# Linear attention and a squared-ReLU FFN on one core: another load order, PE transposes for two batches, and row modes in groups

## The chip, the core and the metric

One core of a Trainium2 chip runs the whole kernel. Its engines work side by side: TensorE (PE in the profile, with PEld for its weight loads), VectorE (DVE), ScalarE (ACT), GpSimd (POOL) and SyncE (SP), the last two also issuing DMAs. The metric is device time in microseconds of one execution, the median of three runs: 383.3 us before (382.87 to 383.75).

## What is computed

```python
def phi(x):
    proj = np.einsum('bhsd,df->bhsf', x, w_phi)
    proj = proj - np.max(np.abs(proj), axis=-1, keepdims=True)
    return np.concatenate([np.exp(proj), np.exp(-proj)], axis=-1)
q_p, k_p = (phi(q), phi(k))
kv = np.einsum('bhsf,bhsd->bhfd', k_p, v)
z = np.sum(k_p, axis=2)
num = np.einsum('bhsf,bhfd->bhsd', q_p, kv)
den = np.einsum('bhsf,bhf->bhs', q_p, z)[..., None] + 1e-06
x = (num / den).transpose(0, 2, 1, 3).reshape(B * S, H * D)
h = np.maximum(x @ w_in, 0.0)
out = h * h @ w_out
```

8 batches, 8 heads, 576 positions, head size 64, 128 features; then 4608 tokens of width 512 through an FFN of width 2048. Inputs and output are float32; the kernel computes in bfloat16 with float32 sums.

## The kernel before

Everything is recorded first as operations of a `Plan` (L46): engine, estimated cost, a key (its priority), the operations that it needs, and the buffers that it takes from rings. `Plan.order` (L78) then walks through estimated time and gives each free engine, among the operations that are ready and find their buffers free, the one with the lowest key. The instructions are written in that order, and each engine runs its own in order. `fill` (L51) puts a warming matmul on PE whenever it has nothing to do before the first transposed tile (`warm`, L321, two matmuls of 128 columns).

Attention runs batch by batch (`attention`, L342). The names, with their lines:

- Loads (L294 to L319): GpSimd issues the DMAs of k, q and v (tiles xk, xq, xv), in halves for batch 0, and of the two FFN weights, win and wout.
- Transposes of k and q to kT and qT (L347): on PE with copies by ScalarE or VectorE (L364, L372, L375) for batch 0 and for k of batch 1, else by DMA from SyncE's queue (L353). NPE at L180 sets which.
- The k side: in five groups, PE projects k (L412), VectorE takes the largest absolute value (mk, L423) and, from batch 1 on, subtracts it (ksh, L433), ScalarE makes both exponentials (kph, L441; in batch 0 L454). In batch 0 v is scaled instead (va, L461 and L467, half on VectorE and half on GpSimd). PE sums kph times va in two halves (L500), which are copied to kv_sb (L513, L517).
- The q side, in blocks of 64 positions, two at a time and at the end of a batch one alone: PE projects (L538, features in rows; L567, positions in rows), ScalarE takes exponentials (qph, L548), VectorE the maximum (m, L571), GpSimd moves it to the place of its rows (mq, L580), ScalarE makes em of it (L587). PE makes numerators and denominators in two steps (L616), with a multiplication by em on VectorE between them (L627); VectorE divides (rden L634, xo L638).
- xo is transposed to xT by PE (L648, L653) in batch 0 and by DMA later (L657).

The FFN runs on chunks of four token tiles of 128: `ffn_in` (L669) makes 512 columns of hidden values with PE (L679), ReLU on ScalarE (hr, L684) and the square on GpSimd or VectorE (L687, L690); `ffn_out` (L699) sums with wout (L708), VectorE copies (ot, L715), SyncE stores (L720). The first chunk's FFN-in units take one tile at a time and then two; all others take four at once (L730 to L740).

Matmuls of the projections and of the sums over k use PE in row halves (64\*128 in the profile, `rows=64` in the plan); the others use all rows. The numerators of a single block write only 64 rows of PSUM (128\*64 in the profile).

Of the kernel before, what the change touches and what calls it, by code (L numbers as in the profile page):

```python
# [45 lines left out]
class Plan:  # L46
# [30 lines left out]

    def order(self):  # L78
# [13 lines left out]
        while True:  # L92
            for e, q in ready.items():
# [3 lines left out]
                while q:  # L97
                    it = heapq.heappop(q)
                    o = it[2]
# [58 lines left out]
def kernel(  # L158
# [10 lines left out]
    nc = tc.nc  # L169
# [10 lines left out]
    NPE = 2  # L180
# [15 lines left out]
    ones = sb.tile([P, Fd], BF16, name="ones")  # L196
# [24 lines left out]
    NATT, LEAD, DUE, SPAN = 6, 3, 34, 28  # L221

# [71 lines left out]
    def loads(b, dep=None):  # L294
        got = {}
        for i, (name, src, r) in enumerate((("k", k, r_xk), ("q", q, r_xq), ("v", v, r_xv))):
            buf = Buf(r)
            rows = src[b].rearrange("h s d -> (h s d)").rearrange(
                "(pr t c) -> t pr c", pr=NPR, t=P)

            def fn(a, z, buf=buf, rows=rows):
                nc.gpsimd.dma_start(
                    out=buf.t[:, a * NJ : z * NJ].rearrange("t (pr j) d -> t pr (j d)", j=NJ),
                    in_=rows[:, a:z, :],
                )
            key = FIRST + i if b == 0 else FIRST + (10, 13, 14)[i] if b == 1 else 32 * b - 120
            cut = (0, 2, 4) if b == 0 else (0, 4)
            got[name] = buf, [[load(key, 295 * (z - a), 128 * (z - a),
                                    lambda a=a, z=z, fn=fn: fn(a, z), [dep], [buf])]
                              for a, z in zip(cut, cut[1:])]  # L310
        return got

    x0 = loads(0)
    o_id = pool(FIRST + 0.5, 700, lambda: make_identity(nc, ident))
    win_v = moe_w_in.rearrange("(kc p) m -> p kc m", p=P)
    wout_v = moe_w_out.rearrange("(kc p) n -> p kc n", p=P)
    o_win = load(FIRST + 5, 4194, 512, lambda: nc.gpsimd.dma_start(out=win, in_=win_v))
    x1 = loads(1)
    o_wout = load(FIRST + 12, 4194, 2048, lambda: nc.gpsimd.dma_start(out=wout, in_=wout_v))  # L319

    def warm():  # L321
        for _ in range(2):
            nc.tensor.matmul(out=r_one.tiles[7][:, :P], lhsT=ones, rhs=ones, start=True, stop=True)  # L323
# [18 lines left out]
    def attention(b, x, key):  # L342

        (xk, lk), (xq, lq), (xv, lv) = x["k"], x["q"], x["v"]
        kT, qT = Buf(r_kT), Buf(r_qT)

        def transposes(xb, ld, xt, at):  # L347

            ops = []
            if b >= NPE or b and at:  # L350
                for u0, n in GRP:
# [5 lines left out]
                    ops.append(xbar(key(at), n * 16, fn, ld[0] + (x["v"][1][0] if b > 1 else []), [xb, xt]))  # L357
# [167 lines left out]
        for i, (g0, j0, nj) in enumerate(order_j):  # L525
# [19 lines left out]
            for bk in range(2):  # L545
                for t, sg in zip(qg, (1.0, -1.0)):
                    def fn(w=w, t=t, sg=sg, nj=nj, bk=bk):
                        nc.scalar.activation(  # L548
                            out=t.t.rearrange("f pr hi p -> f (pr hi p)")[:, : nj * 512].rearrange(
                                "f (r b c) -> f b r c", r=2, b=2)[:, bk],  # L550
                            in_=w[bk].t[:, : nj * 256].rearrange("f (r c) -> f r c", r=2),
                            func=ACT.Exp, scale=sg)
                    qe.append(act(kk, nj * 256, fn, [p_], [w[bk], t]))
# [23 lines left out]
            def move(m0=m0, mq=mq, nj=nj, lo=lo):  # L577
                for jj in range(nj):
                    for hi in range(2):
                        nc.gpsimd.tensor_copy(  # L580
                            out=mq.t[lo + jj * 64 : lo + jj * 64 + 64, :, :, hi],
                            in_=m0.t[hi * 64 : hi * 64 + 64, :, : 2 * nj].rearrange(
                                "x b (r j) -> x r b j", j=nj)[:, :, :, jj])
# [220 lines left out]
```

## Time and profile before

| what | us |
|---|---|
| median of three runs | 383.3 |
| span of the profiled execution, first to last instruction | 382.5 |
| around it, against the median | 0.8 |
| PE busy, of which warming matmuls | 366.7, 24.0 |
| VectorE, ScalarE, GpSimd busy | 247.7, 244.4, 185.9 |
| first FFN-in matmul | 37.45 |
| first FFN-out matmul | 49.49 |

The only profile is that of one execution; its span stands for that execution's time. In rows of the timeline the columns are: start, length, engine, line, operation, tiles written and read, array mode and shapes, count, and in brackets the engine's idle time just before and what ended it. A row's length for several matmuls runs to the modelled end of the last one; the distance between two rows' starts tells what the first one cost PE.

### The profile page before, as it was taken

The page shows a single profiled execution, that of the slowest core. Times are in us where ns is not written, and L with a number is a line of the kernel's source. Part 1 is how long each engine was busy: PE and PEld are TensorE (multiplying, and loading weights), DVE is VectorE, ACT ScalarE, POOL GpSimd, SP SyncE. Part 2 cuts the span into 40 slices and gives each one's busy share as a digit, 9 for nine tenths or more (in the row PEclk, how much of TensorE's full clock was granted, in tenths as well). Part 3 has the DMA queues.
Part 4 walks back from the last instruction along what each step waited for, and adds up shares of the span by engine and source line. Part 5 has one row for each costly group of instructions (what it writes and reads, how often), then busy time and mean ns, then how long its engine had stood idle before and what let it go on. Part 6 is the DMA issues. An engine that isn't in the chain of part 4 may idle for free.

```text
span 382.5 us, 10585 instructions
## 1 busy us (share of the span) xinstructions
PE 366.7 (96%) x4194; PEld 200.9 (53%) x4194; DVE 247.7 (65%) x554; ACT 244.4 (64%) x485; POOL 185.9 (49%) x317
## 2 busy tenths in 40 slices
PE   8989999978999999999999999999999999999994
PEld 8868857544544454545543544455446444444442
DVE  1857894899279738973699488956895843333221
ACT  3785788649972986489758974996399733333300
POOL 8533766507890986079728674677446420000000
PEclk9998999999999999999999999999999999999998
DMA  7999994257944595459665946495631422112123
GB/s 114 213 208 205 162 174 73 48 91 133 195 50 89 91 217 62 80 105 202 99 85 109 169 85 104 91 196 102 105 77 30 71 55 49 35 29 55 27 64 75
DMA packets 70721, 40.41 MB, mean 106 GB/s; under 512 B 51088, under 2 KB 65552, under 8 KB 70672
## 3 DMA queue, kind: packets, MB, share of 16 engines
q1 hardware_dynamic: 55360, 21.38, 31.2%
q0 software_dynamic: 15312, 18.35, 29.4%
q8 instruction: 33, 0.54, 0.6%
q14 instruction: 16, 0.13, 0.1%
HBM read 36.77 MB, written 9.44 MB: 121 GB/s over the span
## 4 chain that ended last, share of the span: by engine, by line
PE 74%; DMA 11%; DVE 9%; issue 3%; POOL 1%; DVEq 0%; POOLq 0%
PE one L708 32%; PE one L679 25%; DMA wout<-in_moe_w_out_dram 8%; PE one L616 5%; PE one L500 5%; DVE mk L423 4%; DVE ksh L433 3%; PE one L538 3%; DMA xv<-in_v_dram 2%; PE one L567 2%; PE one L412 2%; DVE ot L715 1%; DVE xo L638 1%; POOL va L467 1%; DVE one L627 1%
## 5 line engine op out<-in xcount | busy, mean ns | idle before, releaser
L687 POOL TENSOR_TENSOR h<-hr 128x512 bf16<-128x512 bf16 x112 | 115.2, 1042 | 83.7 <-ACT hr L684 81.7
L679 PE MATMUL one<-xT,win 128*128 128x512 bf16 (+2 forms) x704 | 144.2, 341 | 2.8 <-DVE ksh L433 2.8
L708 PE MATMUL one<-wout,h 128*128 128x512 bf16 x576 | 144.5, 380 | 0.8 <-DMA wout<-in_moe_w_out_dram 0.5
L684 ACT ACTIVATE hr<-one 128x512 bf16<-128x512 f32 x144 | 84.5, 603 | 67.7 <-PE one L679 59.8
L548 ACT ACTIVATE qph<-one 128x512 bf16<-128x512 f32 (+1 forms) x160 | 77.9, 563 | 19.5 <-PE one L538 19.3
L679 PEld LDWEIGHTS <-win 128*128 128x128 bf16 x704 | 59.2, 98 | 54.6 <-issue 3.5
L708 PEld LDWEIGHTS <-h 128*128 128x128 bf16 x576 | 51.0, 98 | 56.6 <-issue 1.4
L441 ACT ACTIVATE kph<-ksh 128x1024 bf16<-128x1024 f32 (+1 forms) x70 | 64.8, 964 | 19.7 <-DVE ksh L433 19.2
L571 DVE TENSOR_REDUCE m<-one 128x4 f32<-128x512 f32 (+1 forms) x80 | 47.9, 630 | 41.7 <-PE one L567 24.9
L423 DVE TENSOR_REDUCE mk<-one 128x4 f32<-128x512 f32 (+1 forms) x80 | 49.7, 627 | 8.3 <-PE one L412 8.2
L433 DVE TENSOR_TENSOR ksh<-one,mk 128x512 f32<-128x512 f32 (+1 forms) x70 | 44.7, 638 | 3.8
L715 DVE COPY ot<-one 128x512 f32<-128x512 f32 x36 | 24.7, 685 | 28.2 <-PE one L708 28.0
L580 POOL COPY mq<-m 64x4 f32<-64x4 f32 x144 | 26.5, 184 | 32.0 <-DVE m L571 27.3
L616 PEld LDWEIGHTS <-qph 128*128 128x128 bf16 (+1 forms) x640 | 29.7, 100 | 22.2 <-issue 11.3
L616 PE MATMUL one<-kv_sb,qph 128*128 128x65 bf16 (+1 forms) x640 | 36.9, 196 | 1.5 <-DVE one L627 1.4
L627 DVE TENSOR_TENSOR one<-one,em 128x260 f32<-128x260 f32 (+1 forms) x80 | 31.5, 429 | 5.8 <-PE one L616 2.3
L638 DVE TENSOR_TENSOR xo<-one,rden 128x256 bf16<-128x256 f32 (+1 forms) x80 | 31.7, 419 | 0.8
L690 DVE TENSOR_TENSOR h<-hr 128x512 bf16<-128x512 bf16 x32 | 13.5, 423 | 24.4 <-ACT hr L684 24.4
L323 PE MATMUL one<-ones 128*128 128x128 bf16 x316 | 24.0, 236 | 1.1 <-DVE scrap L281 1.1
L500 PE MATMUL one<-va,kph 64*128 64x65 bf16 x1152 | 22.8, 191 | 0.9 <-issue 0.9
L500 PEld LDWEIGHTS <-kph 64*128 64x128 bf16 x1152 | 20.5, 94 | 4.3 <-issue 3.3
L323 PEld LDWEIGHTS <-ones 128*128 128x128 bf16 x316 | 20.6, 106 | 2.5 <-DVE scrap L281 1.1
(43 smaller groups left out, 184.5 us busy)
## 6 DMA issues: line engine op xcount, KB each, us to landing
out_dram<-ot SPq DMA_DIRECT2D x72, 128.0 KB, 2.4
xk<-in_k_dram POOLq DMA_DIRECT2D x7, 576.0 KB, 6.1
xq<-in_q_dram POOLq DMA_DIRECT2D x7, 576.0 KB, 9.8
xv<-in_v_dram POOLq DMA_DIRECT2D x7, 576.0 KB, 12.2
win<-in_moe_w_in_dram POOLq DMA_DIRECT2D x1, 2048.0 KB, 18.5
wout<-in_moe_w_out_dram POOLq DMA_DIRECT2D x1, 2048.0 KB, 32.4
xk<-in_k_dram POOLq DMA_DIRECT2D x2, 288.0 KB, 5.6
xq<-in_q_dram POOLq DMA_DIRECT2D x2, 288.0 KB, 7.6
```

The costliest lines, as they stand in the source:

```text
L323: nc.tensor.matmul(out=r_one.tiles[7][:, :P], lhsT=ones, rhs=ones, start=True, stop=True)
L423: nc.vector.tensor_reduce(out=mk.t[:, e, ms], in_=wv(e), axis=AX.X, op=ALU.max, apply_absolute_value=True)
L433: nc.vector.tensor_tensor(out=ksh.t[:, e, : n // 2, :], in0=wv(e), in1=mk.t[:, e, ms].to_broadcast([P, n // 2, Fd]), op=ALU.subtract)
L441: nc.scalar.activation(out=t.t[:, :, : n // 2, :].rearrange("x e i f -> x e (i f)"), in_=ksh.t[:, :, : n // 2, :].rearrange("x e i f -> x ...
L500: nc.tensor.matmul(out=kvp(w, hi)[:, 2 * prl + s], lhsT=kph[g][s].t[r, i % 2, i // 2, :], rhs=va[s].t[r, u, : D + 1], start=(j == 0), stop ...
L548: nc.scalar.activation(out=t.t.rearrange("f pr hi p -> f (pr hi p)")[:, : nj * 512].rearrange("f (r b c) -> f b r c", r=2, b=2)[:, bk], in ...
L571: d1 = [dve(kk, nj * 256, lambda w=w, m0=m0, nj=nj, bk=bk: nc.vector.tensor_reduce(out=m0.t[:, bk, : 2 * nj], in_=w[bk].t[:, : nj * 256].r ...
L616: nc.tensor.matmul(out=nd(slice(0, D + 1))[:, z], lhsT=qg[s].t.rearrange("f pr hi p -> f (pr hi p)")[:, h * (hi_ - lo) : (h + 1) * (hi_ - ...
L679: nc.tensor.matmul(out=w.t[:, y * n : (y + 1) * n], lhsT=win[:, kc, mc * P : (mc + 1) * P], rhs=xT.t[:, a:z, kc, :], start=(kc == 0), stop ...
L684: o = act(key - 4, TCH, lambda: nc.scalar.activation(out=r.t, in_=w.t, func=ACT.Relu), [p_], [w, r])
L687: o = pool(key - 4, 1050, lambda: nc.gpsimd.tensor_tensor(out=t.t, in0=r.t, in1=r.t, op=ALU.mult), [o], [r, t])
L708: nc.tensor.matmul(out=w.t, lhsT=h2[c, mc, tt][0].t[:, h2[c, mc, tt][1] :][:, :P], rhs=wout[:, mc, :], start=(mc == 0), stop=(mc == KC2 - 1))
```

## The change

1. The loads are issued in the order k0, v0, q0, win, k1, v1, wout, q1 (the digit is the batch), and later batches in the order k, v, q.
2. NPE becomes a pair, and q of batch 1 is transposed by PE as well.
3. The second chunk's FFN-in units take two token tiles instead of four: first all eight units of its first two tiles, then those of the other two.
4. A new `pick` chooses for PE between operations that use row halves and the others, so that several of one kind follow each other.
5. Numerators of a single block are made for all 128 columns of qph, of which 64 are used; qph is laid out for that.
6. In batch 0 em comes straight from the maxima, with four small ScalarE operations instead of GpSimd's four copies and one.
7. One warming matmul of 256 columns stands for two of 128.

```diff
+    AHEAD, GROUP, LATE = 12, 2, 4
+
+    def pick(self, q, rows, can):
+        now = min((it[0] for it in q if it[2].rows == 128), default=None)
+        half = sorted(it for it in q if it[2].rows == 64 and can(it[2]))
+        if now is None or now < 1 or not half:
+            return None
+        if rows == 64:
+            go = half[0][0] < now + self.AHEAD
+        else:
+            go = half[0][0] < now - self.LATE or (
+                len([it for it in half if it[0] < now]) >= self.GROUP)
+        if go:
+            one = half[0]
+        else:
+            one = min((it for it in q if it[2].rows == 128 and can(it[2])), default=None)
+            if one is None:
+                return None
+        q.remove(one)
+        heapq.heapify(q)
+        return one
...
-                while q:
-                    it = heapq.heappop(q)
-                    o = it[2]
+                one = self.pick(q, rows[e], can) if e == "pe" else None
+                while q or one:
+                    it = one or heapq.heappop(q)
+                    one, o = None, it[2]
...
-    NPE = 2
+    NPE = 2, 2
...
+    EMB = 1
...
+    FIRSTS = "k0 v0 q0 win k1 v1 wout q1"
...
+    def loads(b, dep):
+        for name in "kvq":
+            load_x(b, name, 32 * b - 120, dep)
...
     def warm():
-        for _ in range(2):
-            nc.tensor.matmul(out=r_one.tiles[7][:, :P], lhsT=ones, rhs=ones, start=True, stop=True)
+        nc.tensor.matmul(
+            out=r_one.tiles[7][:, : 2 * Fd], lhsT=ones[:, :P], rhs=ones, start=True, stop=True)
...
-            if b >= NPE or b and at:
+            if b >= NPE[at]:
...
+            if b < EMB:
+                def fn(m0=m0, em=em, nj=nj, lo=lo):
+                    for jj in range(nj):
+                        for hi in range(2):
+                            nc.scalar.activation(
+                                out=em.t[lo + jj * 64 : lo + jj * 64 + 64].rearrange(
+                                    "x (r b hi) -> x r b hi", r=2, b=2)[:, :, :, hi],
+                                in_=m0.t[hi * 64 : hi * 64 + 64, :, : 2 * nj].rearrange(
+                                    "x b (r j) -> x r b j", j=nj)[:, :, :, jj],
+                                func=ACT.Exp, scale=-2.0)
+                o_em = act(key(20), 200, fn, d1, [m0, mq, em])
...
                         nc.tensor.matmul(
-                            out=nd(slice(0, D + 1))[:, z],
-                            lhsT=qg[s].t.rearrange("f pr hi p -> f (pr hi p)")[
-                                :, h * (hi_ - lo) : (h + 1) * (hi_ - lo)],
+                            out=w.t[:, z * P : z * P + D + 1],
+                            lhsT=qg[s].t[:, h // 2, h % 2, :],
...
+        if c == 1:
+            ins = [(0, c, (i, a, a + 2)) for a in (0, 2) for i in range(8)]
```

Three places in the orders of instructions show what moves. The first is GpSimd's queue after its constants, with the first loads; in it L302 and L328 load k, q and v, L317 and L343 load win, L319 and L346 load wout, and L467 and L500 scale v. Before:

```order
L302 DMA xk_69<-in_k_dram 128x2x576 x2
masks.py:197 MEMSET ident 128x128
masks.py:199 ISA
masks.py:199 AFFINE_SELECT ident<-ident 128x128
L302 DMA xq_71<-in_q_dram 128x2x576 x2
L302 DMA xv_73<-in_v_dram 128x2x576 x2
L317 DMA win<-in_moe_w_in_dram 128x4x2048
L302 DMA xk_70<-in_k_dram 128x4x576
L302 DMA xq_72<-in_q_dram 128x4x576
L302 DMA xv_74<-in_v_dram 128x4x576
L467 TENSOR_TENSOR va_91<-xv_73,va_91 128x8x64 x2
L319 DMA wout<-in_moe_w_out_dram 128x16x512
```

and now, from the second half of k0 on:

```order
L328 DMA xk_69<-in_k_dram 128x2x576
L328 DMA xv_73<-in_v_dram 128x2x576 x2
L328 DMA xq_71<-in_q_dram 128x2x576 x2
L343 DMA win<-in_moe_w_in_dram 128x4x2048
L328 DMA xk_70<-in_k_dram 128x4x576
L328 DMA xv_74<-in_v_dram 128x4x576
L500 TENSOR_TENSOR va_91<-xv_73,va_91 128x8x64
L346 DMA wout<-in_moe_w_out_dram 128x16x512
L500 TENSOR_TENSOR va_91<-xv_73,va_91 128x8x64
L328 DMA xq_72<-in_q_dram 128x4x576
```

v0 stands ahead of q0, and q1 behind wout. The second place is VectorE in batch 0, from the second group of k on (L423 and L456 are k's maxima, L372 and L405 copy transposes, L467 and L500 scale v). Before:

```order
L423 TENSOR_REDUCE mk_103<-one_163 128x4
L423 TENSOR_REDUCE mk_103<-one_164 128x4
L372 COPY qT_76<-one_159 128x1024
L372 COPY qT_76<-one_158 128x1024
L467 TENSOR_TENSOR va_90<-xv_73,va_90 128x8x64 x2
L423 TENSOR_REDUCE mk_103<-one_159 128x4
L423 TENSOR_REDUCE mk_103<-one_161 128x4
```

and now:

```order
L456 TENSOR_REDUCE mk_103<-one_163 128x4
L456 TENSOR_REDUCE mk_103<-one_164 128x4
L500 TENSOR_TENSOR va_90<-xv_73,va_90 128x8x64
L456 TENSOR_REDUCE mk_103<-one_162 128x4
L500 TENSOR_TENSOR va_90<-xv_73,va_90 128x8x64
L456 TENSOR_REDUCE mk_103<-one_158 128x4
L405 COPY qT_76<-one_160 128x1024
L456 TENSOR_REDUCE mk_103<-one_161 128x4
L500 TENSOR_TENSOR va_90<-xv_73,va_90 128x8x64
L405 COPY qT_76<-one_164 128x1024
```

The third group's maxima (one_159 and one_161 before, one_162 and one_158 now) stand ahead of q's copies. The third place is PE in batch 1, at the first numerators of a single block (L616 before, L661 now; each pair of rows is one matmul with its weight load). Before:

```order
L616 LDWEIGHTS qph_99
L616 MATMUL one_161<-kv_sb_93,qph_99 64x65
L616 LDWEIGHTS qph_99
L616 MATMUL one_161<-kv_sb_93,qph_99 64x65
L708 LDWEIGHTS h_129
L708 MATMUL one_162<-wout,h_129 128x512
```

and now, from the same stretch of PE's order, the transposes of q1 behind an FFN-in, and a little later such a block's numerators:

```order
L723 LDWEIGHTS win
L723 MATMUL one_162<-xT_119,win 128x256
L723 LDWEIGHTS win
L723 MATMUL one_162<-xT_119,win 128x256
L397 LDWEIGHTS xq_72
L397 MATMUL one_161<-ident,xq_72 128x128
```

```order
L661 LDWEIGHTS qph_101
L661 MATMUL one_162<-kv_sb_95,qph_101 128x65
L661 LDWEIGHTS qph_101
L661 MATMUL one_162<-kv_sb_95,qph_101 128x65
L723 LDWEIGHTS win
L723 MATMUL one_158<-xT_119,win 128x256
```

The output of a single block's numerators has 128 rows now instead of 64, and the transposes of q1 (xq_72) are on PE, behind FFN-in matmuls of 256 columns.

96 lines of the change are left out of this document (50 added, 46 removed).

## The prediction, made before the changed kernel ran

> **What bounds the kernel now.** I read the page first (busy time by engine, the slices, the costliest groups), then windows by stage, then PE's timeline where PE isn't full.
>
> ```profile
> PE 366.7 (96%) x4194; PEld 200.9 (53%) x4194; DVE 247.7 (65%) x554; ACT 244.4 (64%) x485; POOL 185.9 (49%) x317
> PE   8989999978999999999999999999999999999994
> ...
> L323 PE MATMUL one<-ones 128*128 128x128 bf16 x316 | 24.0, 236 | 1.1 <-DVE scrap L281 1.1
> ```
>
> PE is busy 96% of the span, but 24.0 us of that are the warming matmuls of L323, which compute nothing and all stand ahead of the first FFN matmul or just beside it. From there on PE does real work with few gaps. The windows show where the gaps are.
>
> ```profile
> 20.00:30.00 10.00, 8.13 (x231) 6.70 (x229) 5.44 (x10) 7.63 (x22) 2.74 (x9) 0.93 1.15 207
> 40.00:50.00 10.00, 8.83 (x169) 7.88 (x168) 9.57 (x23) 7.20 (x14) 8.05 (x14) 1.00 1.25 163
> 82.00:93.00 11.00, 7.65 (x66) 3.54 (x63) 10.64 (x22) 8.88 (x12) 4.87 (x7) 1.00 0.57 103
> 160.00:200.00 40.00, 38.81 (x449) 19.63 (x448) 28.32 (x66) 28.91 (x56) 24.64 (x41) 1.00 0.72 119
> 200.00:240.00 40.00, 39.05 (x453) 19.21 (x451) 31.67 (x73) 29.94 (x59) 27.49 (x44) 1.00 0.65 115
> ```
>
> The columns are the window and its length, then PE, PEld, DVE, ACT and POOL busy, the granted clock, the DMA share and GB/s. In 40 to 50 and in 82 to 93 VectorE is full (9.57 of 10, 10.64 of 11) and PE isn't (1.2 and 3.35 us idle): there VectorE sets the pace. In 160 to 240 PE is idle for 2.1 of 80 us.
>
> ```profile
> 27.63 0.38 PE L567 MATMUL one<-wphi,qT 64*128 64x128 bf16 x7 [1.87 <-ACT qph L548]
> ...
> 37.45 1.06 PE L679 MATMUL one<-xT,win 128*128 128x128 bf16 x16
> ...
> 49.49 1.02 PE L708 MATMUL one<-wout,h 128*128 128x512 bf16 x4 [0.49 <-DMA wout<-in_moe_w_out_dram]
> ...
> 83.87 0.62 PE L616 MATMUL one<-kv_sb,qph 128*128 128x65 bf16 x8 [1.42 <-DVE one L627]
> ```
>
> So the time has three parts: a start of 37.45 us until the first FFN matmul, PE's real work from there, and waits inside that work. The profiled span is 382.5 us, 0.8 under the median of 383.3; I work out a difference and carry it from the span to the median.
>
> **Term 1, PE's own work: -3.9 us.** PE runs in three array modes: 128\*128, 64\*128 (row halves) and 128\*64 (the numerators of single blocks).
>
> ```profile
> 52.72 0.31 PE L616 MATMUL one<-kv_sb,qph 128*64 128x65 bf16 x4
> 52.96 1.04 PE L708 MATMUL one<-wout,h 128*128 128x512 bf16 x4
> 53.93 0.31 PE L616 MATMUL one<-kv_sb,qph 128*64 128x65 bf16 x4
> ...
> 105.41 0.29 PE L616 MATMUL one<-kv_sb,qph 128*128 128x65 bf16 x4
> 105.53 1.02 PE L679 MATMUL one<-xT,win 128*128 128x512 bf16 x4
> 106.39 0.54 PE L616 MATMUL one<-kv_sb,qph 128*128 128x65 bf16 x12
> ...
> 202.66 1.04 PE L679 MATMUL one<-xT,win 128*128 128x512 bf16 x4
> 203.63 0.40 PE L412 MATMUL one<-wphi,kT 64*128 64x128 bf16 x8
> ```
>
> Start to start, four FFN matmuls take 0.86 us when a full-width numerator follows (105.53 to 106.39), but 0.97 ahead of a 128\*64 one (52.96 to 53.93) and 0.97 ahead of a 64\*128 one (202.66 to 203.63). A change of mode costs about 0.10 us. Counted along PE's two orders from the first FFN matmul on, the changes fall from 233 to 176: 57 at 0.10 are -5.7. All of that is the narrow mode; changes into and out of row halves stay nearly as many (179 to 176), because the second chunk's FFN-in comes in twice as many pieces. Four narrow numerators take 0.24 with their change of mode, so 0.14 without, against 0.12 at full width: 128 of them, -0.6. Against that, 34 more transposes stand behind the first FFN matmul (18 of q1, 16 of k1): at 0.06 (16 matmuls of this size in the row at 37.45 take 1.06 us) +2.0; four more output transposes and the shorter FFN matmuls +0.4. Sum -3.9.
>
> The Trainium skill, TensorEngine Tiling (Array Packing), section Performance Considerations, speaks against giving the narrow mode up: it advises column tiling where the stationary side has 64 columns or fewer, for up to twice the speed. By that rule 128 matmuls would take twice as long, an estimate of +3.8 us from the 0.12 us of four. The trace doesn't agree: here the narrow ones aren't faster at all.
>
> **Term 2, the start: -6.0 us.** ScalarE's chain decides when the first transposed tile is there.
>
> ```profile
> 9.90 0.59 ACT L454 ACTIVATE kph<-one 128x512 bf16<-128x512 f32 x1
> ...
> 16.69 1.08 ACT L454 ACTIVATE kph<-one 128x512 bf16<-128x512 f32 x2 [2.14 <-DVE mk L423]
> ...
> 25.56 0.39 ACT L513 ACTIVATE kv_sb<-one 128x260 bf16<-128x260 f32 x1 [0.88 <-PE one L500]
> ...
> 29.48 1.09 ACT L548 ACTIVATE qph<-one 128x512 bf16<-128x512 f32 x2 [1.49 <-PE one L538]
> ...
> 34.84 0.60 ACT L548 ACTIVATE qph<-one 128x512 bf16<-128x512 f32 x1 [3.21 <-PE one L538]
> 35.33 0.59 ACT L653 ACTIVATE xT<-one 128x512 bf16<-128x512 bf16 x1
> ```
>
> From 9.90 to the end of the xT copy (35.92) are 26.0 us, 7.7 of them idle (2.14 + 0.88 + 1.49 + 3.21), so 18.3 of work. The work stays, but for em: four small operations instead of one, and GpSimd's copies gone. No row has the small form; two of the old one take 0.29 in the row below, one alone 0.22 by its mean, so the second adds 0.07 to 0.1 and a block about 0.3 (bounds 0.2 and 0.7), 0.6 for the two blocks ahead of xT.
>
> ```profile
> 41.82 0.29 ACT L587 ACTIVATE em<-mq 128x8 f32<-128x8 f32 x2
> ...
> 13.90 2.15 DVE L467 TENSOR_TENSOR va<-xv,va 128x512 bf16<-128x512 bf16 x2 [0.20 <-DMA xv<-in_v_dram]
> ...
> 4.82 8.99 DMA xv<-in_v_dram
> ```
>
> The first half of v lands at 13.81 (4.82 + 8.99), and VectorE's next reductions stand behind the work on it and behind q's copies: that makes the 2.14. Loaded second, v lands where q's first half did, about 3 us sooner, and VectorE reduces the third group ahead of q's copies. Walking the new orders engine by engine with these durations I get the last exponential of k at 21.3, the first numerators at 24.5 and the end of the xT copy at 29.2, with 0.85 us of ScalarE idle. I add 1.2 for hops between engines that a walk leaves out, and 1.1 for the numerators that PE has ahead of the first FFN matmul: 31.5 instead of 37.45. Bounds: 29.9, if all idle time goes (9.90 + 18.3 + 0.6 + 1.1), and 37, if the idle time comes back elsewhere and only PE's work between xT and FFN shrinks.
>
> **Term 3, VectorE behind the start: +4.5 us.** Batch 1's k side begins earlier, but its pace is VectorE's.
>
> ```profile
> 41.73 0.69 DVE L423 TENSOR_REDUCE mk<-one 128x4 f32<-128x512 f32 x1
> ...
> 43.06 0.68 DVE L423 TENSOR_REDUCE mk<-one 128x4 f32<-128x512 f32 x1
> ...
> 57.55 0.42 DVE L433 TENSOR_TENSOR ksh<-one,mk 128x256 f32<-128x256 f32 x1
> ...
> 63.09 0.76 DVE L571 TENSOR_REDUCE m<-one 128x2 f32<-128x256 f32 x2 [4.13 <-PE one L538]
> ```
>
> A reduction with its subtraction takes 1.33 us, and batch 1's ten pairs, with what is mixed in, filled 16.2 us (41.73 to 57.97). The new order mixes in 1.5 us more (two of kT's copies, more of batch 0's numerators), and PE's transposes of q1 add three copies behind. It starts at 36.7 and ends its last subtraction at 54.4. PE's work up to its first FFN-out is 12.3 us, so to 43.8; but the fourth output tile is multiplied out only after 10.6 us of VectorE, at 47.3. PE waits 3.8 us up to there, then 1.2 for the third group's exponentials and 0.7 for the fifth's: 5.7, against 1.2 before. Bounds of the wait: 0 and 10, as my walk is too loose or too tight. wout is hidden: it came for 49.49, and with q1 behind it 576 KB at the 207 GB/s of 20 to 30 make 2.8 us less, so it is there by 46.7, ahead of the first FFN-out near 47.8. The five transposes of q1 by DMA, which were under way beside it, are gone as well.
>
> **Term 4, batch 2's k side: -2.3 us.** Of the 3.35 us that PE idled in 82 to 93 I keep 1.0 (bounds 0 and 4): FFN-in on pairs of tiles gives PE 11.1 us of work between the first projection and the sums over k, and VectorE comes there with less backlog, since the wait of 4.13 us for q's projection goes with the DMA transposes.
>
> Sum: -3.9 - 6.0 + 4.5 - 2.3 = **-7.7**, a span of 374.8 and a time of **375.6 us**. Behind batch 2 I cost the new order at nothing: VectorE and ScalarE are busy some 70 to 80% in 160 to 240. The warming matmuls, one over 256 columns for two over 128, fill only idle time.
>
> **The rivals.** (a) *VectorE is no wall*: PE waits in term 3 as little as before, 371.1 us. For it: VectorE's 4.13 us of slack right behind. Against: 9.57 of 10 in 40 to 50. 15%.
>
> (b) *The clock halves*. The wait of 1.87 us that ended at 27.63 was followed by this:
>
> ```profile
> 28.00:30.00 2.00, 2.00 (x24) 1.39 (x24) 1.29 (x2) 0.52 (x2) 0.55 (x3) 0.63 1.22 208
> 30.00:32.00 2.00, 2.00 (x26) 2.00 (x25) 0.87 (x2) 1.63 (x5) 1.68 (x3) 0.52 1.21 209
> ```
>
> The granted clock of 0.63 and 0.52 over 2 us each is 1.7 us lost. Term 3's waits have no warming matmuls to cover them. One such stretch in PE's real work gives 377.3, three give 380.7 us. Against it: the waits in 82 to 93 left the clock at 1.00. 13%. The Trainium skill, TensorE: Matmul & The Clock Gate, Part 1, has the clock fall after an idle window of about 3.4 us; by it only the 3.8 us of wait, if it comes in one piece, would count. The trace is stricter: 1.87 us were enough.
>
> (c) *The start hardly moves*: the first FFN matmul at 37, so 5.5 us more than forecast, 381.1 us. 12%.
>
> (d) *Slower, by bursts*: the new order puts projections of two or three groups in a row (in batch 4 20 matmuls, then 12 of FFN, then the sums). VectorE needs 2.7 us for each group; 12 FFN matmuls cover 2.6. If every batch from 2 to 7 then waits like batch 2 did, 3.3 us, that is 19.8 where about 3 are in the sum (1.0 here, the 2.1 of 160 to 240): 392.4 us. The total turns slower than before at 1.8 us for each batch. For it: PE did wait for VectorE where groups stood close. Against: in most batches 5 us or more of PE's work lie between a group and its sum. 10%.
>
> (e) *It doesn't do what it says*: row modes are hardly grouped by the count above, and if the other terms cancel, nothing is left. 5%.
>
> **How the numbers follow.** My forecast has 45%, with 373 to 378.5 as its own range. It and (a) to (c) are faster, 0.85; (e) is same, 0.05; (d) slower, 0.10. The border is 0.2% (0.8 us), about what a measurement can tell. The range 369.5 to 382.5 holds (a) to (c) and the bounds of terms 3 and 4, and leaves out (d), (e) and a little below (a).
>
> **What would show it.** The first FFN matmul at about 31.5 and the first FFN-out near 48, with no wait for wout (terms 2, 3); no 128\*64 matmuls, and 0.86 us for four FFN matmuls ahead of any numerators (term 1); PE's waits between 38 and 56 named after VectorE or ScalarE; under 1.5 us of wait in batch 2's k side (term 4). Granted clocks under 1.00 behind 40 us speak for (b), waits for ksh in every batch for (d). I am wrong if the first FFN matmul comes after 35, or if PE waits over 10 us between it and batch 2.

## The result, and the profile after

The changed kernel takes **371.66 us** (median of four runs, 370.68 to 372.0), the kernel before in the same comparison 383.52 us (382.87 to 384.66): a ratio of 0.9682, 95% interval 0.966 to 0.9703. The forecast was 375.6 us in a range of 369.5 to 382.5. The profiled execution took 371.88 us, 369.8 of them between its first and last instruction; before it was a span of 382.5. Where time and span of one execution of the kernel before are both on record, the time is 1.7 to 1.9 us longer, so its profiled execution took some 384.3 us, 0.8 more than the median. Of the 12.7 us between the two spans 0.8 belong to that execution; the medians differ by 11.9.

From the page of the changed kernel, the busy time by engine and the group of the warming matmuls:

```profile
PE 359.0 (97%) x4103; PEld 202.4 (55%) x4103; DVE 251.2 (68%) x557; ACT 246.7 (67%) x498; POOL 182.3 (49%) x299
...
L355 PE MATMUL one<-ones 128*128 128x256 bf16 x143 | 21.8, 302 | 1.2 <-DVE scrap L305 1.2
```

From its windows, the five stretches of which the prediction showed the rows before (window, length, then PE, PEld, DVE, ACT and POOL busy, granted clock, DMA share, GB/s):

```profile
20.00:30.00 10.00, 9.85 (x178) 6.75 (x177) 8.12 (x18) 9.78 (x30) 3.07 (x4) 1.00 1.14 207
40.00:50.00 10.00, 7.06 (x120) 5.43 (x117) 9.79 (x26) 7.20 (x10) 5.50 (x6) 1.00 1.21 208
82.00:93.00 11.00, 10.74 (x153) 7.00 (x152) 8.62 (x16) 10.54 (x18) 7.75 (x13) 1.00 0.54 92
160.00:200.00 40.00, 40.00 (x520) 20.73 (x512) 31.14 (x70) 31.96 (x61) 27.33 (x45) 1.00 0.81 128
200.00:240.00 40.00, 39.93 (x461) 20.68 (x460) 31.21 (x68) 30.51 (x60) 25.50 (x42) 1.00 0.70 126
```

The stretch from 40 to 50 got worse: PE idles 2.9 us, 1.2 before, with VectorE full in both. The other two got better: 0.26 us idle in 82 to 93 where 3.35 were, and 0.07 of 80 where 2.1 were in 160 to 240. The granted clock is 1.00 throughout.

PE's timeline of the changed kernel shows where the new waits lie:

```profile
31.81 1.05 PE L723 MATMUL one<-xT,win 128*128 128x128 bf16 x16
...
41.60 0.63 PE L661 MATMUL one<-kv_sb,qph 128*128 128x65 bf16 x8 [0.81 <-DVE ksh L466]
43.26 0.28 PE L661 MATMUL one<-kv_sb,qph 128*128 128x65 bf16 x4 [1.03 <-DVE ksh L466]
...
48.14 0.28 PE L692 MATMUL one<-ident,xo 128*128 128x128 bf16 x2 [0.82 <-DVE xo L682]
```

The first FFN matmul starts at 31.81 instead of 37.45; behind it PE waits for VectorE. What PE waited for once that is over stands in its list of waits (what waited, for whom, us in total, times, longest). Before, from 56 us on:

```profile
PE one L679 <- DVE ksh L433: 2.8, 5, 0.7
PE one L616 <- DVE one L627: 1.4, 1, 1.4
PE one L500 <- issue: 0.9, 1, 0.9
...
```

Six lines, 5.9 us in all. After, from 56 us on, the list has one line:

```profile
PE one L723 <- DVE ksh L466: 0.6, 2, 0.3
```

With PE's time cut at three points (first FFN matmul, end of batch 1's k side, last matmul) the whole difference can be accounted for. The windows of before:

```profile
37.45:59.00 21.55, 20.38 (x287) 15.73 (x285) 19.75 (x45) 17.03 (x30) 13.83 (x19) 1.00 1.10 157
59.00:377.70 318.70, 312.61 (x3276) 155.41 (x3274) 205.93 (x467) 203.90 (x398) 152.81 (x263) 1.00 0.53 94
```

and of after:

```profile
31.81:56.00 24.19, 20.44 (x380) 16.63 (x377) 21.46 (x51) 19.39 (x38) 12.08 (x12) 1.00 0.98 167
56.00:365.10 309.10, 308.40 (x3295) 163.36 (x3290) 209.22 (x469) 203.79 (x399) 153.59 (x263) 1.00 0.54 97
```

| us | before | after | difference | forecast |
|---|---|---|---|---|
| first FFN matmul | 37.45 | 31.81 | -5.6 | -6.0 |
| PE busy from there (sum of both windows) | 332.99 | 328.84 | -4.15 | -3.9 |
| PE idle up to the end of batch 1's k side | 1.17 | 3.75 | +2.6 | +4.5 |
| PE idle behind it | 6.09 | 0.70 | -5.4 | -2.3 |
| behind the last matmul | 4.8 | 4.7 | -0.1 | 0 |
| span | 382.5 | 369.8 | -12.7 | -7.7 |

### The profile page after: what moved, and what is told of

Its sections match the earlier page's. It is cut to its first block, busy times and chain, and to the rows that moved or that the text cites. A ratio compares the mean times of both kernels' runs of the same rounds, so it can differ in the third digit from the quotient of the medians.

```text
span 369.8 us, 10380 instructions
## 1 busy us (share of the span) xinstructions
PE 359.0 (97%) x4103; PEld 202.4 (55%) x4103; DVE 251.2 (68%) x557; ACT 246.7 (67%) x498; POOL 182.3 (49%) x299
## 4 chain that ended last, share of the span: by engine, by line
PE 79%; DVE 11%; DMA 3%; issue 2%; ACT 2%; POOL 1%; DVEq 0%; POOLq 0%
PE one L752 32%; PE one L723 28%; PE one L661 5%; DVE mk L456 5%; PE one L533 4%; DVE ksh L466 4%; PE one L571 3%; DMA xq<-in_q_dram 3%; PE one L600 3%; PE one L355 2%; PE one L445 1%; ACT qph L581 1%; DVE xo L682 1%; DVE one L671 1%; ACT em L614 0%
## 5 line engine op out<-in xcount | busy, mean ns | idle before, releaser
L752 PE MATMUL one<-wout,h 128*128 128x512 bf16 x576 | 145.0, 380 | 0.1
L723 PEld LDWEIGHTS <-win 128*128 128x128 bf16 x768 | 65.5, 98 | 49.3 <-issue 1.7
L752 PEld LDWEIGHTS <-h 128*128 128x128 bf16 x576 | 51.3, 98 | 56.2 <-issue 1.5
L456 DVE TENSOR_REDUCE mk<-one 128x4 f32<-128x512 f32 (+1 forms) x80 | 49.8, 627 | 9.2 <-PE one L445 8.2
L661 PEld LDWEIGHTS <-qph 128*128 128x128 bf16 x640 | 30.4, 97 | 18.4 <-issue 4.5
L661 PE MATMUL one<-kv_sb,qph 128*128 128x65 bf16 x640 | 35.2, 194 | 2.0 <-DVE ksh L466 1.8
L625 POOL COPY mq<-m 64x4 f32<-64x4 f32 x126 | 23.3, 185 | 10.4 <-DVE m L604 6.3
L355 PE MATMUL one<-ones 128*128 128x256 bf16 x143 | 21.8, 302 | 1.2 <-DVE scrap L305 1.2
L678 DVE RECIPROCAL rden<-one 128x4 f32<-128x4 f32 (+1 forms) x80 | 12.6, 175 | 10.4 <-PE one L661 10.1
## 6 DMA issues: line engine op xcount, KB each, us to landing
xq<-in_q_dram POOLq DMA_DIRECT2D x7, 576.0 KB, 11.9
```

What stands on the lines that cost most here:

```text
L456: nc.vector.tensor_reduce(out=mk.t[:, e, ms], in_=wv(e), axis=AX.X, op=ALU.max, apply_absolute_value=True)
L661: nc.tensor.matmul(out=w.t[:, z * P : z * P + D + 1], lhsT=qg[s].t[:, h // 2, h % 2, :], rhs=kv[r][0].t[:, z % 2, z // 2, s, :], start=(s ...
L723: nc.tensor.matmul(out=w.t[:, y * n : (y + 1) * n], lhsT=win[:, kc, mc * P : (mc + 1) * P], rhs=xT.t[:, a:z, kc, :], start=(kc == 0), stop ...
L752: nc.tensor.matmul(out=w.t, lhsT=h2[c, mc, tt][0].t[:, h2[c, mc, tt][1] :][:, :P], rhs=wout[:, mc, :], start=(mc == 0), stop=(mc == KC2 - 1))
```

## The experiments

Each takes one part of the change back, or tests one cost. In the five comparisons the kernel before measured between 382.5 and 383.5 us, so a difference of a microsecond between kernels of different comparisons says little. In the traces of all kernels but before and after, 41 to 49 of the 576 matmuls of the FFN-out line have no record; lines like "L752 <- issue: 1.4, 9, 0.2" are these gaps and no waits, and busy sums there are some microseconds low. I therefore go by named waits and times.

| run | what differs from the changed kernel | changes of mode | us | ratio to before, 95% |
|---|---|---|---|---|
| (the changed kernel) | | 176 | 371.66 | 0.966 to 0.9703 |
| e1_no_pick | no grouping of row modes | 208 | 375.13 | 0.9783 to 0.9821 |
| e2_no_pairs | chunk 1 on four tiles | 170 | 377.32 | 0.9846 to 0.9883 |
| e3_q1_dma | q1 transposed by DMA | 200 | 397.09 | 1.0344 to 1.0404 |
| e4_old_loads | old order of kinds in the loads | 183 | 376.37 | 0.9809 to 0.9862 |
| e5_narrow | narrow numerators | 218 | 376.62 | 0.9817 to 0.9853 |
| e6_em_pool | em by way of GpSimd | 172 | 371.82 | 0.9689 to 0.976 |
| e7_q1_dma_no_pick | e3 and e1 together | 210 | 408.58 | 1.0614 to 1.0722 |
| e8_pick_alone | kernel before, grouping added | 225 | 382.96 | 0.9967 to 1.0038 |
| e9_kcopy_act | two copies of kT from VectorE to ScalarE | 180 | 372.99 | 0.9685 to 0.9756 |
| e10_q1_dma_late | e3, loads released later | 200 | 388.93 | 1.0106 to 1.0185 |
| e11_early_loads | loads released earlier | 176 | 394.14 | 1.0233 to 1.031 |
| e12_start_alone | e1, e2 and e5 together | 242 | 379.74 | 0.9886 to 0.9937 |

### Changes of PE's mode: e1_no_pick, e5_narrow, e8_pick_alone

```diff
-                one = self.pick(q, rows[e], can) if e == "pe" else None
+                one = None
```

> The changed kernel without its choice between row modes (PE takes the lowest key, as before). Changes of mode on PE from the first FFN matmul on: 208 instead of 176. Theory A, the choice is worth its mode changes only: 32 x 0.095 = 3.0 us, so 374.7 us against 371.7, and PE's waits behind batch 2 stay as small as in the changed kernel (0.1 us idle in 160 to 240). Theory B, the choice also took away the late waits for VectorE (2.1 us idle in 160 to 240 before): 2 us more, 376.5 to 377, and such waits are back. Theory C, neither matters because the planner makes up for it elsewhere: 371 to 372.5.

Measured: 375.13 us, 3.5 more for 32 changes of mode more, 0.11 us each (0.09 by the spans of the two profiled executions, 372.8 and 369.8; 0.14 by the ratios to the kernel before). Behind 56 us no wait over 0.3 us comes back, so the price of the changes is what the grouping saves: theory A.

In e5_narrow the numerators of a lone block write 64 columns again:

```diff
-                            out=w.t[:, z * P : z * P + D + 1],
-                            lhsT=qg[s].t[:, h // 2, h % 2, :],
+                            out=nd(slice(0, D + 1))[:, z],
+                            lhsT=qg[s].t.rearrange("f pr hi p -> f (pr hi p)")[
+                                :, h * (hi_ - lo) : (h + 1) * (hi_ - lo)],
```

> The changed kernel with the numerators of a lone token block 64 columns wide again, as before. TensorE then changes its mode 218 times (168 of rows, 50 of columns) and not 176. Theory A (a change of columns costs like a change of rows, 0.095 us, and a 64-column matmul gains little): 42 x 0.095 = 4.0 and 0.6 for the matmuls themselves, 375.7 to 376.5 us. Theory B (only changes of rows cost): 8 fewer of those, 370.9 to 372.3 us.

Measured: 376.62 us, 5.0 more, 0.1 over theory A's range; B is out. Up to 1.7 of the 5.0 belong to a stretch of half clock that the profiled execution had and the changed kernel's had not, as its windows show:

```profile
44.00:46.00 2.00, 2.00 (x26) 2.00 (x24) 1.83 (x7) 1.80 (x3) 1.01 (x2) 0.50 1.22 212
46.00:48.00 2.00, 2.00 (x30) 1.74 (x29) 1.09 (x5) 0.60 (x1) 0.94 (x2) 0.74 1.21 204
```

The granted clock of 0.50 and 0.74 over 2 us each loses 1.0 and 0.5 us, and 0.90 in the 2 us ahead of them another 0.2. With 0.6 us for the narrow matmuls themselves a change costs between 0.06 and 0.10 us here. The changed kernel's own timeline shows the price directly:

```profile
200.72 1.02 PE L752 MATMUL one<-wout,h 128*128 128x512 bf16 x4
201.68 0.40 PE L600 MATMUL one<-wphi,qT 64*128 64x128 bf16 x8
202.01 1.04 PE L752 MATMUL one<-wout,h 128*128 128x512 bf16 x4
202.88 1.03 PE L723 MATMUL one<-xT,win 128*128 128x512 bf16 x4
```

Four FFN matmuls take 0.96 us ahead of row halves (200.72 to 201.68) and 0.87 ahead of others (202.01 to 202.88): 0.09 a change.

e8_pick_alone puts `pick` alone into the kernel before.

> The kernel before with the grouping of row modes alone added. TensorE changes its mode 225 times and not 233. Theory A (the grouping is worth its changes of mode only): 8 x 0.095 = 0.8, 381.2 to 382.5 us, with 2 us idle between 160 and 240 us as before and 3 us between 82 and 93. Theory B (the grouping also mends the waits behind batch 2): 378 to 380.5 us, with under 0.7 us idle between 160 and 240 us.

Measured: 382.96 us against 382.91 for the kernel before beside it, where theory A has 381.2 to 382.5: no gain that can be told. On the old list of work the grouping finds only 8 changes to save, and PE's list of waits from 56 us on is as long as before (the gaps of missing records left out):

```profile
PE one L523 <- issue: 1.9, 1, 1.9
PE one L435 <- DVE ksh L456: 1.3, 2, 0.9
PE one L702 <- DVE mk L446: 1.1, 1, 1.1
...
```

With the smaller ones it is 6.1 us. The first line is a single wait of another kind, which comes up at e4.

### The start: e4_old_loads, e6_em_pool, e9_kcopy_act

```diff
-    FIRSTS = "k0 v0 q0 win k1 v1 wout q1"
+    FIRSTS = "k0 q0 v0 win k1 q1 v1 wout"
```

> The changed kernel with the load order of before (k0 q0 v0 win k1 q1 v1 wout). 183 mode changes instead of 176 (+0.7 us). Theory A, v's early landing is what started the FFN early: first FFN matmul at 34 to 36 instead of 31.8, and 373.5 to 376 us. Theory B, the start gain came from the new PE order and the direct em, and VectorE sets the pace until 55 us anyway: first FFN matmul at 32 to 33, 371.5 to 373 us.

Measured: 376.37 us, 0.4 over theory A's range; the first FFN matmul starts at 34.06, 2.25 later, as theory A has it. But v's landing is not what delays it. ScalarE waits 0.97 us for k's maxima, in the changed kernel 0.94, and begins q's exponentials at 21.75, there at 22.12. The delay comes behind that, with a wait of PE for which the profile names no releaser ("issue"):

```profile
26.78 0.40 PE L571 MATMUL one<-qT,wphi 64*128 64x256 bf16 x4 [1.78 <-issue]
```

ScalarE waits 1.73 us for these matmuls. The trace has a 16 KB transfer of instructions (queue q8) from 24.47 to 25.43, and PE goes on 1.35 us after it; the section on the hardware has the other cases. Behind the start there is also a longer wait for VectorE, which ended in a half clock:

```profile
52.38 0.71 PE L661 MATMUL one<-kv_sb,qph 128*128 128x65 bf16 x8 [1.77 <-DVE one L671]
...
55.02 1.50 PE L752 MATMUL one<-wout,h 128*128 128x512 bf16 x4
```

Four FFN-out matmuls take 1.44 us at 55.02 (to 56.46), 0.87 at full clock. The later start, this wait and the half clock together come near the difference of 4.7. What the order of the first loads is worth at the start is therefore not shown: 1.73 of the 2.25 us are PE's wait, and whether the load order brought that about is open.

```diff
-    EMB = 1
+    EMB = 0
```

> The changed kernel with batch 0's em made as in the other batches, by four copies on GpSimd and one exponential on ScalarE, and not by four small exponentials on ScalarE (0.21 us each). Theory A (ScalarE sets the first FFN matmul, which takes 31.8 now): it starts at 31.2 or before, and the time is 370.6 to 371.5 us. Theory B (the detour over GpSimd is on the way to batch 0's numerators and their division): the first FFN matmul starts at 32.3 or later, and the time is 372.2 to 373.5 us.

Measured: 371.82 us, between the two ranges, while the first FFN matmul starts at 30.98, 0.83 us earlier. Theory A is right on the place: the four small exponentials do delay the start. In the median nothing is left of it; in the profiled execution 0.5 us is (a span of 369.3 for 369.8), and the rest went into later waits, none over 0.5 us behind 56 us. The four times spread from 370.77 to 373.08 us, so theory A's sum is neither borne out nor refuted. The small exponentials take 0.21 us each in the changed kernel's groups by shape:

```profile
L614 ACT ACTIVATE em<-m 64x4 f32<-64x4 f32 x18 | 3.7, 207 | 0.3
```

In e9 VectorE is relieved of two copies, 0.96 us, in the middle of the stretch in which PE waits for it:

```diff
-                if b or at:
+                if at or b and u0 == 0:
                     o = dve(kk, n * 38, lambda w=w, n=n, ms=ms: nc.vector.tensor_copy(
```

> The changed kernel with the second and third copy of batch 1's transposed k (0.68 and 0.28 us) on ScalarE and not on VectorE. Theory A (VectorE's throughput sets TensorE's 5.5 us of waits between 37 and 56): the first FFN-out matmul starts at 48.3 or before instead of 48.93, the last subtraction of batch 1 ends by 54.5 instead of 55.2, and the time is 370.4 to 371.4 us. Theory B (what VectorE gains, ScalarE loses, whose exponentials hold the same banks): no earlier first FFN-out, 371.5 to 373 us.

Measured: 372.99 us, the top of theory B's range. VectorE does get done earlier: the last subtraction of batch 1 ends at 54.2 instead of 55.2, as theory A has it, and from 28 to 56 us PE idles 3.15 us instead of 3.75 (one wait of 1.38 us for a product of VectorE stands where the two of 0.81 and 1.03 were). But the first FFN-out matmul starts at 48.80 instead of 48.93, no earlier to speak of, and behind 56 us there are 1.4 us of named waits where 0.6 were, with four more changes of mode. So the two copies do delay VectorE, but that its throughput alone sets the time is not borne out.

### Chunk 1 on pairs: e2_no_pairs, and three parts at once: e12_start_alone

```diff
-        if c == 1:
-            ins = [(0, c, (i, a, a + 2)) for a in (0, 2) for i in range(8)]
```

> The changed kernel with the second chunk's FFN-in on four tiles at once again. 170 mode changes instead of 176 (-0.6 us). Theory A, the pairs are what covers batch 2's k side: PE waits 3 to 4 us for VectorE there again (82 to 93 before: 3.35 us), 374 to 375 us. Theory B, VectorE's earlier start already covers it: 371 us, PE's wait there under 1 us.

Measured: 377.32 us, above both. In the stretch that the two theories are about, theory B is right: in batch 2's k side PE waits 0.77 us, and in e12, which has no pairs either, 0.33. The pairs are not needed to end that wait.

```profile
88.35 1.02 PE L723 MATMUL one<-xT,win 128*128 128x512 bf16 x4 [0.77 <-DVE ksh L466]
```

The time is lost elsewhere. PE's timeline shows a wait that the changed kernel does not have, far from chunk 1:

```profile
206.79 0.27 PE L600 MATMUL one<-wphi,qT 64*128 64x128 bf16 x3
209.01 0.33 PE L600 MATMUL one<-wphi,qT 64*128 64x128 bf16 x5 [1.95 <-issue]
...
209.55 1.78 PE L723 MATMUL one<-xT,win 128*128 128x512 bf16 x4
```

1.95 us of wait, and the four FFN matmuls behind it take 1.58 us (to 211.13) instead of 0.87: the wait is paid twice. No releaser is named here either; an instruction transfer of 16 KB ran from 206.65 to 207.62, beside a batch's loads, and PE goes on 1.4 us after it. Both theories had counted only the stretch that the edit touches; the edit changes the order of the whole list, and the waits of later batches with it.

e12_start_alone undoes the pairs, the grouping and the full-width numerators together.

> The changed kernel with three parts undone at once: no grouping of row modes, chunk 1's FFN-in on four tiles, narrow numerators. What is left is the new load order, q of batch 1 on TensorE and em on ScalarE. 242 changes of mode, 66 more. Theory A (the parts are worth their work on TensorE, and the start, VectorE's wait and the end of the wait at batch 2 belong to what is left): 371.7 + 66 x 0.095 + 0.6 = 378.5, 377.5 to 380 us. Theory B (each part undone costs what it cost alone, 3.5 + 5.7 + 5.0 in e1_no_pick, e2_no_pairs and e5_narrow): 384.5 to 387 us, so no gain on the kernel before is left.

Measured: 379.74 us, 8.1 over the changed kernel: theory A. So the parts undone one by one (3.5, 5.7 and 5.0 us, a sum of 14.2) overstate what they are worth together. What is left in this kernel (load order, q1 on PE, em on ScalarE, the one warming matmul) is 3.7 us faster than the kernel before beside it (383.41), although it changes mode 9 times more. Its waits from 56 us on:

```profile
PE one L753 <- issue: 1.4, 9, 0.2
PE one L724 <- DVE ksh L466: 0.6, 2, 0.3
PE one L533 <- issue: 0.4, 1, 0.4
PE one L753 <- DVE ksh L466: 0.3, 1, 0.3
PE one L724 <- ACT qph L581: 0.2, 1, 0.2
```

Without the first line, the gaps of missing records, that is 1.5 us where before has 5.9.

### q of batch 1 by DMA: e3, e7, e10, and the loads alone: e11

```diff
-    NPE = 2, 2
+    NPE = 2, 1
```

> The changed kernel with q of batch 1 transposed by DMA as before. 200 mode changes instead of 176 (+2.3 us by the planner's other order), 18 transposes (1.0 us of PE) and 1.5 us of VectorE copies less. Theory A, the DMA transposes collide with wout and come late, VectorE idles for them: 373.5 to 376 us, with VectorE idle for 3 us or more before batch 1's q side. Theory B, moving q1 to PE was worth nothing or cost a little, VectorE being the limit there: 370 to 372 us.

Measured: 397.09 us, far over both. The start is unchanged (first FFN matmul at 31.82); most of the loss lies behind 100 us. PE's waits there, and the time from issue to landing of all DMA transposes of xT:

```profile
PE one L723 <- DMA xT<-xo: 13.9, 3, 7.3
```

```profile
DMA to landing us min/median/max: 2.4/2.4/12.1
```

In the changed kernel the same view says

```profile
DMA to landing us min/median/max: 2.4/2.4/5.5
```

The chain that ended last in e3 (start, us, what) goes through one of them:

```profile
197.35 0.59 PE one L752 x2
...
198.03 12.15 DMA xT<-xo
...
210.32 1.86 PE one L723 x4
```

The three loads of a later batch (1.7 MB) were issued at 194.40 to 196.69 and landed by 209.89: the transpose was issued into them and landed when they had. The loads of a batch are released by a gate that waits for the transposes of q of the batch before. In e3 these gates come earlier: at 83.4, 116.2 and 150.4 us, in the changed kernel at 88.0, 125.8 and 164.6, in stretches in which hardly any xT is to be transposed. Ten transposes of xT were issued while loads moved, four in the changed kernel. Is it the place of the loads, the grouping, or the DMA transposes of q themselves? First the grouping, taken out of e3:

> The changed kernel with q of batch 1 transposed by DMA, as in e3_q1_dma (397.1 us), and with the grouping of row modes taken out, as in e1_no_pick (375.1 us). Theory A (the 25 us of e3_q1_dma came from the order that the grouping makes of that list of work, with FFN units set ahead of the attention that feeds them): the time is that of e1_no_pick within 2 us, 373.5 to 377 us, and TensorE idles under 3 us between 160 and 240 us. Theory B (the DMA transposes of q of batch 1 cost it themselves, through the queue that they share): 393 us or more, with 10 us idle or more in that stretch.

Measured: 408.58 us, theory B's range. The grouping is not the cause; theory A falls. 15 transposes of xT fall into loads, with a median of 4.2 us to landing over all 32.

Then e3 with the gate planned later (1000 becomes 7000 in the plan), and the changed kernel with the gate on k's transposes instead of q's:

```diff
-            d = pl.op("x", 1000, key(2), None, tq)
+            d = pl.op("x", 1000, key(2), None, tk)
             gates[b] = pool(key(2), 100, lambda: nc.gpsimd.tensor_copy(
-                out=gate, in_=qT.t[:1, M - 1, P - 8 :]), [d], [qT])
+                out=gate, in_=kT.t[:1, M - 1, P - 8 :]), [d], [kT])
```

> The kernel of e3_q1_dma (q of batch 1 transposed by DMA, 397.1 us) with the gate that releases a batch's three loads planned 6 us later; nothing else is edited, and 200 changes of mode stay. Theory A (the 25 us came from the loads of batches 3 to 6, released while the output tiles were still to be transposed by DMA: ten of those were issued into the loads and took 7 to 12 us where others take 2.4): at most four output transposes fall into the loads, TensorE waits under 3 us for them, and the time is 372 to 379 us. Theory B (DMA transposes of q of batch 1, or the order of TensorE that follows from them, cost it): 390 us or more.

Measured: 388.93 us, just outside B's bound and far from A's. The delay took the collisions only from ten to nine, of which six took over 5 us instead of nine, with waits of 4.9 us for xT instead of 13.9, and the time fell by 8 us; the edit did not do what theory A needed, and does not decide alone.

> The changed kernel with the gate that releases a batch's loads bound to the transposes of k and not of q, so that the loads of batches 3 to 7 are issued some 4 to 14 us earlier; q of batch 1 stays on TensorE, and 176 changes of mode stay. Theory A (loads that run beside the output tiles' DMA transposes hold these up, and TensorE with them): six or more output transposes take over 5 us, and the time is 378 to 400 us. Theory B (earlier loads do no harm): 370 to 373.5 us.

Measured: 394.14 us: theory A. Here q1 is on PE and the changes of mode are 176 as in the changed kernel; the loads of batch 4 are issued at 112.33 instead of 126.97, and 13 transposes of xT fall into loads. PE's waits, the landing times of xT, and a piece of the chain:

```profile
PE one L723 <- DMA xT<-xo: 7.9, 3, 6.0
PE one L600 <- DMA qT<-xq: 5.8, 2, 3.9
```

```profile
DMA to landing us min/median/max: 2.4/3.7/11.1
```

```profile
119.56 8.14 DMA xT<-xo
...
127.83 3.57 PE one L723 x8
```

The eight FFN matmuls behind the wait take 3.57 us, 1.75 at full clock. That early loads alone bring a loss of this kind is shown. That they are all of e3's 25 us is not: its own DMA transposes and its other order of PE were never had without them.

## Why the prediction was right, and where its sizes were off

The sign and the range held, and each term came with its sign, but not in the forecast order of size: term 3, second with +4.5, is the smallest with +2.6. The span came out 5.0 us lower than the forecast 374.8, and the time of 371.66 us lies below 373 to 378.5, the forecast's own range; what held is the wide range, which took in the rivals. The reasons given for terms 2 and 4 stand only in part, so there the sizes came out with some luck. The 0.8 us that carry the span to the median compare two executions: the profiled one was slower than the median.

**Term 1, PE's own work** (-3.9, measured -4.15). The price of 0.10 us a change holds: 0.09 in the changed kernel's timeline, 0.09 to 0.14 in e1, 0.06 to 0.10 in e5. The statement that the narrow mode buys nothing holds too: with it back the time is 5.0 us longer. By the rule in the Trainium skill, TensorEngine Tiling (Array Packing), section Performance Considerations, which favours column tiling for 64 stationary columns, e5 should have been faster; the measurement says otherwise. The numerators of a lone block all use the same column half, though, so narrow matmuls in both halves at once are not tested here. What the count hid is that row changes "stay nearly as many": the grouping does save 32 of them, as e1 shows, on a list that the pairs and the other parts would have made longer.

**Term 2, the start** (-6.0, measured -5.6). First FFN matmul at 31.81 for 31.5. The walk had em at 0.3 us more for a block; four operations of 0.21 take 0.85, 0.63 more than the old one's 0.22 and near the upper bound of 0.7; without them (e6) the first FFN matmul starts 0.83 us earlier. The walk's other steps were too long by some 0.4 us in all.

The reason given for the term holds only in part. ScalarE's 7.7 us of idle time did shrink to 0.94, but the wait for mk, which the prediction put down to v's landing and q's copies, only from 2.14 to 0.94, and with the old load order (e4) it is 0.97. The larger waits, 1.49 and 3.21 us, were waits for PE. They came behind PE's wait of 1.87 us and the half clock that followed it, which the prediction used for the clock alone. That wait splits one projection of eight matmuls; the first is

```profile
25.55 0.22 PE L567 MATMUL one<-wphi,qT 64*128 64x128 bf16 x1
```

and the other seven are the row at 27.63. The profile puts it down to ScalarE, but the weight loads of the seven have no releaser, and an instruction transfer of 16 KB ran from 25.30 to 26.26. The three kernels with such a wait in the start (before, e8, e4) are those whose first FFN matmul comes latest, at 37.45, 36.97 and 34.06; in all others it comes between 30.98 and 32.23. How much of the 5.6 us is the absence of that wait, and which part of the change removed it, no run tells.

**Term 3, VectorE behind the start** (+4.5, measured +2.6). The mechanism is there, named in the profile: waits for ksh and xo between 40 and 49. The size was off by 1.9: 3.75 us of idle PE, not 5.7, since the waits that the walk expected behind the first FFN-out for the exponentials did not come; the last subtraction ended at 55.2 for 54.4. wout landed at 41.8 and was hidden, as said. e9 shows that VectorE's throughput is part of the term: relieved of 0.96 us there, PE idles 0.6 less, and nothing of it reaches the time.

**Term 4, batch 2's k side** (-2.3, measured 0.26 us idle for 3.35, so -3.1). The size is close: 1.0 us was kept and 0.26 is left. Of the two reasons given, the work that the pairs give PE was not needed, since without pairs the wait does not come back (e2, e12). The other, VectorE's smaller backlog without the DMA transposes of q1, fits e3 and e10, where PE waits 2.1 us for ksh in this stretch again, but not e7, where it is 0.5. What ended the wait stays open.

**"Behind batch 2 I cost the new order at nothing"** is the largest miss: the 2.1 us of idle PE in 160 to 240 went to 0.07, and with some pieces elsewhere that is 2.3 us. They did not go with the grouping alone (e8 keeps 6.1 us of named waits behind 56 us). They went with the parts left in e12, whose waits are 1.5 us. Of these the order of the first loads (e4: 0.5 us) and em (e6: 1.5 us) can each be undone without bringing them back, and every kernel with q1 by DMA has 5 us or more (3.5 to 4.3 in e3, e7 and e10 without the waits for DMAs). That points to q of batch 1 on PE, and to the order that the planner makes from it. It is no proof: e2, with q1 on PE too, has 4.2 us of waits, 2.0 of them in one place, and the order k, v, q of the later batches' loads and the one warming matmul were undone in no run. How the edit reaches batches 4 and 5 is argued and not shown: the gates that release later loads hang on q's transposes.

**The rivals.** (a), VectorE no wall, gave 371.1 us and is nearest to the time, but not for its reason: PE did wait in term 3, and the missing microseconds came from behind. (b), the clock, did not happen in this execution, 1.00 throughout, yet the margin is small: two waits of the same length, 0.8 and 1.03 us with 0.63 us of matmuls between them, were followed by a half clock in e5, e7, e10 and e11. (c), a start that hardly moves, is out. (d), bursts that make VectorE late in every batch, did not happen. (e), nothing left, is out. No rival had what would have made the kernel slower: the loads' place. By e11 that lies 22 us away, behind one edit of the release.

## What to carry to other kernels

An edit of a list that a planner orders moves waits in all later stages; undo it alone and in company before crediting it, and count the waits by name over the whole span, not only in the stretch that the edit touches. Look where bulk loads start against the small DMAs on which the critical engine waits: here loads released 9 to 19 us too early cost twice what the whole change brought. Changes of the array's mode are worth counting, at 0.1 us each.

## What the runs showed of the hardware

A DMA transpose issued while a batch's 1.7 MB of loads from GpSimd's queue move took up to 12 us to land: a median of 8 for the 38 of e3, e7 and e11, 2.4 to 5.5 for the four of the changed kernel, which fall into the last 5 us or so of the loads. For the others the median is 2.4.

The clock can fall after less idle time in one piece than the 1.87 us that the prediction found. PE's timeline of e11, at a place where PE's work is that of the changed kernel:

```profile
41.30 0.63 PE L661 MATMUL one<-kv_sb,qph 128*128 128x65 bf16 x8 [0.81 <-DVE ksh L466]
42.95 0.28 PE L661 MATMUL one<-kv_sb,qph 128*128 128x65 bf16 x4 [1.03 <-DVE ksh L466]
43.07 1.05 PE L723 MATMUL one<-xT,win 128*128 128x128 bf16 x16
43.96 0.56 PE L661 MATMUL one<-kv_sb,qph 128*128 128x65 bf16 x8
44.34 1.90 PE L723 MATMUL one<-xT,win 128*128 128x128 bf16 x16
```

Sixteen matmuls take 0.89 us at 43.07 (to 43.96) and 1.69 at 44.34 (to 46.03), and no single wait is longer than 1.03 us. In the changed kernel the same two waits, at 41.60 and 43.26, left the clock at 1.00, as they did in e1, e2, e3 and e12; in e5, e7 and e10 it fell as in e11. Whether they cost anything differs between executions that have the same waits. The Trainium skill, TensorE: Matmul & The Clock Gate, Part 1, has the clock fall after an idle window of about 3.4 us, which runs free, so that the point of change depends on where in the window the work falls. The trace agrees with the variation; no wait at this place is as long as the window.

PE seems to wait for its instructions at times. In before (27.63), e8 (27.14 and 101.54), e4 (26.78) and e2 (209.01) PE goes on 1.3 to 1.5 us after a 16 KB instruction transfer on queue q8 has landed, having waited 1.8 to 2.6 us, each time while bulk loads moved. Most of the 31 to 33 such transfers of a run have no such wait behind them. That these are waits for instructions is argued from the times; no run tests it.
